# Moving zero fills and a weight rounding out of the step from keys to queries, squares in halves, and one rounding handed to VectorE

## The chip, the cores and the metric

One core of a Trainium2 chip runs the whole program. The metric is device time in microseconds of one execution, from the runs listed below. TensorE (PE) does the matrix products, ScalarE (ACT) and VectorE (DVE) move and transform results out of PSUM, GpSimd (POOL) computes squares and issues indirect transfers, SyncE (SP) issues the direct transfers from one queue in order.

## The reference, cut to what matters

Three stages follow each other. The inputs are float32; q, k, v are (4, 8, 576, 64), omega is (128, 64).

```python
def phi(x):                      # x = q or k times 64 ** -0.25
    proj = np.einsum('bhsd,md->bhsm', x, omega)
    sq = np.sum(x * x, axis=-1, keepdims=True) / 2.0
    h = proj - sq
    h = h - np.max(h, axis=-1, keepdims=True)
    return np.exp(h) / np.sqrt(m)
kv = einsum('bhsm,bhsd->bhmd', phi(k), v);  z = sum(phi(k), axis=2)
x  = (phi(q) @ kv) / (phi(q) . z + 1e-6)    # attention: 2304 tokens x 512
# mixture of 8 experts: each token goes to its best expert, gate from a softmax
out[mask] = gate_w[mask, None] * (np.maximum(x[mask] @ w1[e], 0.0) @ w2[e])
# feed-forward, 512 -> 2048 -> 512, with softplus between
g = np.maximum(h, 0.0) + np.log1p(np.exp(-np.abs(h)))
return g @ w_out
```

## The kernel before, in words

**Attention in items.** The four batches are worked through in two pairs (`bp` 0 and 1). Within a pair all keys come first, then all queries, each in five items of up to 256 token rows per batch (`nr` 2; the item with `r == 8` has `nr` 1), so there are 20 items: 0 to 4 keys and 5 to 9 queries of pair 0, 10 to 14 keys and 15 to 19 queries of pair 1. The loop over `n` (22 steps of four slots) works on item `n` and on what is left of item `n - 1`. For an item, `squares` forms x*x and folds it to half the sum of squares on POOL, one item ahead (L454 the squares, L457 six foldings with adds, L463 to L465 the scaling). `transposes` (called with `g4` 0 for the first four heads and, for `nr` 2, with 1 for the last four) turns x on PE, rounds it to the fast float format on ACT (L492, the part called xh) and takes the remainder on DVE (L499, xl). `project` makes three matmuls per block (L510, L513, L514), `features` takes the maximum on DVE (L529 for queries, L532 for keys, and L533, which joins it with the squares) and the exponential on ACT (L535). Keys then go into `k_chunk` (L564, L569), queries into `q_transpose` (L617, L619) and `q_product` (L634, then L655 to L666 on DVE, which write the token tile `xt`, of which there are two). The key items of a pair end with `kv_out`, `kv_transpose` and `kv_gate`; this stretch, in which pair 1 goes from keys to queries (`n` 14 to 16), is called the passage below.

**Routing.** `route_pick`, `route_gate` and `route_rank` follow each query item two steps later; `route_gate` stores the token rows to the DRAM table `x_tok` (L719, L725), POOL scatters token numbers into `id_slot` (L819). The two last query items (the tail) are also handed to expert 0 in SBUF: `route_gate` rounds them (L714, L715), `first_tail` and `first_split` build the transposed input of expert 0 (L767 to L792).

**Zero fills.** `clear_y` writes zeroes to parts of `x_tok` and to the whole of `y_comp` from one SBUF strip, 25 transfers from SP (L300), each waiting for `it.started`, the last projection matmul of item `n`; the kernel before calls it at `n` 12.

**First weights.** The weights come in units of 512 KB. `load_raw` fetches units 0, 1 and 4 (at `n` 12 and 13, L237). `round_raw` (ACT, L247) and `rest_of_raw` (DVE, L252) split a unit into a rounded part and a remainder. Before, unit 0 is split at step 15, units 1 and 4 are rounded at step 20 and their remainders taken at the end of `first_split`. Later units go through `fetch_unit` and `split_unit` (L260, L266, L269).

**Experts and feed-forward.** `places` computes on DVE which expert stands where (L1103 to L1133); SP reads its result into registers to address the gather of expert 1 (L975, L979). `moe_expert` runs two layers per expert (L966 to L968, L1041, L1042), the feed-forward follows (L1230 to L1270). From there to the end PE is busy almost without a break.

**What sets the order.** Each engine executes its own instructions in a fixed order. The framework plans that order when the program is built, by the program's order and by when its own model of the chip has an instruction's inputs ready; so an edit can also move instructions that it does not name. `behind(ins, other)` adds the demand that `ins` comes after `other` on its engine; `latest["DVE"]` holds the last DVE instruction that such a demand should refer to. `at(step, slot, fn, ...)` puts a call into a later step of the loop.

Of the kernel before, what the change touches and what calls it, by code (L numbers as in the profile page):

```python
# [10 lines left out]
F32 = mybir.dt.float32  # L11
# [4 lines left out]
AF = mybir.ActivationFunctionType  # L16
ALU = mybir.AluOpType
# [12 lines left out]
def tile_favor_moe_softplus(  # L30
# [14 lines left out]
    nc = tc.nc  # L45
# [195 lines left out]
            reason="the transfer waits for its turn")  # L241
        return raw

    latest, first_raw = {}, []

    def round_raw(i, raw, last):
        ins = nc.scalar.activation(ring[i % NRING][:, 0:1024], raw, AF.Copy)  # L247
# [41 lines left out]
    with ExitStack() as actx:  # L289
# [157 lines left out]
        def squares(it):  # L447
            src = xin[it.bp, it.kind][it.r // 4][:, :, it.r % 4:it.r % 4 + it.nr, :]
            x2 = wk.tile([P, H, it.nr, D], F32, tag="x2", bufs=1, name="x2")
            if it is items[0]:  # L450
                for h in range(0, H, 4):
                    nc.scalar.activation(x2[:, h:h + 4], src[:, h:h + 4], AF.Square)
            else:
                nc.gpsimd.tensor_tensor(x2, src, src, op=ALU.mult)  # L454
                n = D // 2
                while n:
                    nc.gpsimd.tensor_tensor(x2[:, :, :, 0:n], x2[:, :, :, 0:n], x2[:, :, :, n:2 * n],  # L457
                                            op=ALU.add)
                    n //= 2
                it.sq = sm.tile([P, H, it.nr], F32, tag="sq", bufs=4, name="sq")  # L460
                up = sm.tile([P, H, it.nr], F32, tag="up", bufs=2, name="up")
                whole = x2[:, :, :, 0]
                nc.gpsimd.tensor_scalar(it.sq, whole, 0.5 * SCALE * SCALE, None, op0=ALU.mult)  # L463
                nc.gpsimd.tensor_scalar(up, it.sq, LNM, None, op0=ALU.add)
                nc.gpsimd.tensor_tensor(it.sq, up, it.sq, op=ALU.subtract)  # L465
            it.x2 = x2
# [17 lines left out]
        def transposes(it, g4):  # L484
            flat = xin[it.bp, it.kind][it.r // 4].rearrange("p h r d -> p (h r d)")
            tp = ps.tile([P, 4, P], F32, tag="tp", bufs=2, name="tp")
            for j in range(4):
                blk = 4 * g4 + j
                c0 = (blk * 4 + it.r % 4) * D if it.nr == 2 else 2 * blk * D
                latest["PE"] = nc.tensor.transpose(tp[:, j, :], flat[:, c0:c0 + P], ident)  # L490
            xh = wk.tile([P, 4, P], F32R, tag="xT", name="xT")
            ins = nc.scalar.activation(xh, tp, AF.Copy, scale=SCALE)  # L492
            if it is items[1] and g4 == 0:
                behind(ins, first_done[0])

            k0 = DM * (1 + lows[0] % 3)
            lows[0] += 1
            xl = ring[15][:, k0:k0 + DM].rearrange("p (j t) -> p j t", j=4)
            nc.vector.scalar_tensor_tensor(xl, tp, SCALE, xh.bitcast(F32), op0=ALU.mult,  # L499
                                           op1=ALU.subtract)  # L500
            it.xT[g4] = xh, xl
# [202 lines left out]
        def route_gate(it):  # L704
            n = it.nr
            ex = sm.tile([P, 2, E], F32, tag="ex", name="ex")[:, 0:n]
            nc.scalar.activation(ex, it.dl, AF.Exp)
            gw = it.xg[:, 0:n, DM]
            nc.vector.tensor_reduce(gw, ex, axis=AX.X, op=ALU.add)
            nc.vector.tensor_scalar(gw, gw, 1e-9, None, op0=ALU.add)  # L710
            nc.vector.reciprocal(gw, gw)
            for i, t in enumerate(it.tiles if it in tail else ()):
                x, g = it.xg[:, i, 0:DM], it.xg[:, i, DM:DM + 1]
                nc.scalar.activation(tail_h[t], x, AF.Copy, scale=g)  # L714
                nc.vector.scalar_tensor_tensor(tail_l[t], x, g, tail_h[t].bitcast(F32),  # L715
                                               op0=ALU.mult, op1=ALU.subtract)
            if n == 2:
                t0 = (2 * it.bp + it.r // 4) * S
                nc.sync.dma_start(  # L719
                    x_tok[t0:t0 + 512, :].rearrange("(p r) d -> p r d", r=4)[  # L720
                        :, it.r % 4:it.r % 4 + 2, :], it.xg)
            else:
                for g in range(2):
                    t0 = (2 * it.bp + g) * S
                    nc.sync.dma_start(x_tok[t0 + 512:t0 + S, :], it.xg[g * 64:(g + 1) * 64, 0, :])  # L725
# [48 lines left out]
        def first_split():  # L774

            xh, xl = (ring[i][:, 0:KD * NBLK].rearrange("p (k n) -> p k n", k=KD)
                      for i in (11, 15))
            n = CAPS[0]
            tp = tp_0
            diags = wk.tile([P, H * 2 * D], F32, tag="x2", bufs=1, name="diags")  # L780
            for c in range(NC):
                w = min(P, n - c * P)
                diag = diags[:, c * P:c * P + w]
                nc.gpsimd.tensor_scalar(diag, ident[:, 0:w], xg_0[:, c, DM:DM + 1], None,
                                        op0=ALU.mult)
                for kk in range(KD):
                    nc.tensor.matmul(tp[kk][:, c * P:c * P + w],
                                     lhsT=xg_0[:, c, kk * P:(kk + 1) * P], rhs=diag,
                                     start=False, stop=c == NC - 1)
            for kk in range(KD):  # L790
                nc.scalar.activation(xh[:, kk, 0:n], tp[kk][:, 0:n], AF.Copy)
                latest["DVE"] = nc.vector.tensor_tensor(  # L792
                    xl[:, kk, 0:n], tp[kk][:, 0:n], xh[:, kk, 0:n].bitcast(F32), op=ALU.subtract)
            for args in first_raw:
                rest_of_raw(*args)
            return xh, xl

        def route_rank(it):
# [50 lines left out]
        def at(step, slot, fn, *a):  # L849
            late.setdefault((step, slot), []).append((fn, a))  # L850
# [12 lines left out]
        for n in range(NI + 2):  # L863
# [46 lines left out]
                loads(1)  # L910
            if n == 2:
                clear_ids(it.started)
            if n == 12:
                clear_y(it.started)
            if n == 10:
                loads_q(1)
            for i in UNITS_AT.get(n, ()):
                raw = load_raw(i, it.started)
                if i:
                    at(NI, 3, round_raw, i, raw, True)  # L920
                    first_raw.append((i, raw, True))
                else:
                    at(NI - 5, 0, round_raw, i, raw, True)
                    at(NI - 5, 1, rest_of_raw, i, raw, False)
            if n == NI - 2:

                a, b = (inp.tile([P, VO], F32, tag="kf", bufs=2, name="tail") for _ in range(2))
# [172 lines left out]
    def places():  # L1100

        key = tb.tile([P, E], F32, tag="over", name="key")
        nc.vector.scalar_tensor_tensor(key, cntb, float(E), iota_e, op0=ALU.mult,  # L1103
                                       op1=ALU.subtract)

        def rows(a):
            return a.rearrange("p (o e) -> p o e", o=1).to_broadcast([P, R, R])

        def cols(a):
            return a.rearrange("p (e o) -> p e o", o=1).to_broadcast([P, R, R])  # L1110

        more = tb.tile([P, R, R], F32, tag="sel", name="more")
        nc.vector.tensor_tensor(more, rows(key[:, 1:E]), cols(key[:, 1:E]), op=ALU.is_gt)
        rank = tb.tile([P, R], F32, tag="we", name="rank")
        nc.vector.tensor_reduce(rank, more, axis=AX.X, op=ALU.add)
        at_place = tb.tile([P, R, R], F32, tag="past", name="at_place")
        nc.vector.tensor_tensor(at_place, rows(rank), cols(iota_e[:, 0:R]), op=ALU.is_equal)
        nc.vector.tensor_tensor(more, at_place, rows(iota_e[:, 1:E]), op=ALU.mult)
        nc.vector.tensor_reduce(eid[:, 1:E], more, axis=AX.X, op=ALU.add)
        nc.vector.tensor_copy(eid_i[:, 0, :], eid)  # L1120
        nc.vector.tensor_scalar(eid_i[:, 1, :], eid, float(NT), None, op0=ALU.mult)
        nc.vector.tensor_tensor(more, at_place, rows(cntb[:, 1:E]), op=ALU.mult)
        nc.vector.tensor_copy(cntp[:, 0:1], cntb[:, 0:1])
        nc.vector.tensor_reduce(cntp[:, 1:E], more, axis=AX.X, op=ALU.add)

        off = tb.tile([P, E + 1], F32, tag="off", name="off")
        nc.vector.memset(off[:, E:E + 1], float(NT))
        mc = tb.tile([P, E], F32, tag="nwin", name="mc")
        nc.vector.tensor_tensor(mc, cntp, caps, op=ALU.min)
        for e in reversed(range(E)):  # L1130
            nc.vector.tensor_tensor(off[:, e:e + 1], off[:, e + 1:e + 2], mc[:, e:e + 1],
                                    op=ALU.subtract)
        nc.vector.tensor_copy(off_i, off[:, 0:E])  # L1133
# [283 lines left out]
```

## Time and profile before

| what | value |
|---|---|
| time, median of 3 runs | 845.51 us (845.38 to 845.65) |
| time of the profiled execution | 852.04 us |
| its span, first to last instruction | 850.3 us |
| mean granted TensorE clock in it | 0.991 |
| PE busy | 823.5 us (97% of the span) |
| DVE, ACT, POOL busy | 490.9, 475.9, 222.5 us |

The profile is of one execution; the three runs of the median were taken without it. Busy time of PE counts matmuls and can hide small gaps, since they are pipelined. Where a line of the trace has a bracket, it gives how long the engine stood idle before the instruction and which instruction ended that. The token rows stored by L719 and L725 are named in it by the tile, `x_tok<-xt`; the zero fills are `x_tok<-w` and `y_comp<-w`.

### The profile page before, as it was taken

The numbers are of one execution on the slowest core, as the hardware profiler recorded it, in microseconds if no ns is written. First come the engines' busy times: TensorE is split into PE (matmuls) and PEld (weight loads), VectorE is DVE, ScalarE is ACT, GpSimd is POOL, SyncE is SP. The second block draws the span as 40 slices with busy tenths as digits, with TensorE's granted clock in tenths as the row PEclk, the third lists the DMA queues.
The fourth block names the chain that finished last, engine by engine and source line by source line (L and its number), as shares of the span: only waits on it lengthen the run. The fifth ranks groups of instructions, "written<-read, shape, count | busy, mean of one in ns | idle before, by whom it ended". The sixth has DMA issues, their size and how long they took to land.

```text
span 850.3 us, 14078 instructions
## 1 busy us (share of the span) xinstructions
PE 823.5 (97%) x5127; PEld 763.8 (90%) x5129; DVE 490.9 (58%) x1056; ACT 475.9 (56%) x1053; POOL 222.5 (26%) x361
## 2 busy tenths in 40 slices
PE   8998998998999999999999999999999999999995
PEld 6897998987999999999999999999999999999994
DVE  6678976786787677777678666542232223222221
ACT  4686757763564455566555655565455446445442
POOL 6886889223111011101035333211001001001001
PEclk9999998999999999999999999999999999999998
DMA  9962277024896888889853321030001000000001
GB/s 224 225 180 68 72 156 242 26 69 109 263 292 214 267 255 245 278 253 306 277 185 101 124 79 45 1 112 38 1 5 70 1 1 38 1 0 38 1 1 39
DMA packets 83307, 104.21 MB, mean 123 GB/s; under 512 B 16904, under 2 KB 62632, under 8 KB 83234
## 3 DMA queue, kind: packets, MB, share of 16 engines
q1 hardware_dynamic: 79442, 93.35, 36.8%
q0 software_dynamic: 3792, 9.92, 3.5%
q8 instruction: 42, 0.69, 0.4%
q14 instruction: 31, 0.25, 0.1%
HBM read 78.68 MB, written 24.58 MB: 121 GB/s over the span
## 4 chain that ended last, share of the span: by engine, by line
PE 49%; issue 35%; DMA 7%; DVE 3%; POOL 3%; ACT 2%; SPq 1%; POOLq 0%; ACTq 0%; DVEq 0%
PE a L966 6%; PE a L968 6%; PE a L967 6%; PE y L967 4%; PE y L968 4%; PE y L966 4%; PE nm L634 4%; DMA raw<-in_moe_w_dram 2%; PE kvacc L564 2%; PE o L1253 2%; PE o L1251 2%; PE o L1248 2%; POOL out_dram L1268 2%; DMA y_comp<-w 2%; PE tq L617 2%
## 5 line engine op out<-in xcount | busy, mean ns | idle before, releaser
L1236 DVE SCALAR_TENSOR_TENSOR ab<-a,ab 128x384 f32<-128x384 f32 x96 | 53.4, 556 | 161.8 <-ACT ab L1235 151.1
L966 PE MATMUL a<-yh,w 128*128 128x384 f32 x384 | 129.6, 337 | 0.0
L968 PE MATMUL a<-yh,w 128*128 128x384 f32 x384 | 129.5, 337 | 0.0
L967 PE MATMUL a<-yl,w 128*128 128x384 f32 x384 | 129.0, 336 | 0.0
L1253 PE MATMUL o<-w,gl 128*128 128x512 f32 x288 | 114.0, 397 | 0.0
L1251 PE MATMUL o<-w,gh 128*128 128x512 f32 x288 | 113.9, 396 | 0.0
L1248 PE MATMUL o<-w,gh 128*128 128x512 f32 x288 | 112.9, 393 | 0.1
L1233 ACT ACTIVATE ab<-a 128x384 f32<-128x384 f32 x96 | 47.1, 491 | 113.0 <-PE a L968 112.9
L269 DVE TENSOR_TENSOR w<-raw,w 128x1024 fp32r<-128x1024 f32 x69 | 84.2, 1222 | 26.6 <-ACT w L266 25.9
L535 ACT ACTIVATE ph<-pj,nb 128x128 f32<-128x128 f32 x288 | 82.2, 395 | 30.0 <-DVE nb L533 21.0
L266 ACT ACTIVATE w<-raw 128x1024 fp32r<-128x1024 f32 x69 | 72.8, 1057 | 37.6 <-DMA raw<-in_moe_w_dram 37.3
L1268 POOL DMA_INDIRECT out_dram<-ob,idx x18 | 17.6, 976 | 280.7 <-ACT ob L1266 277.2
L1240 DVE TENSOR_TENSOR gl<-ab,gh 128x384 fp32r<-128x384 f32 x96 | 60.6, 631 | 52.1 <-ACT gh L1239 52.1
L1239 ACT ACTIVATE gh<-ab 128x384 fp32r<-128x384 f32 x96 | 50.4, 525 | 54.0 <-DVE ab L1236 53.7
L967 PE MATMUL y<-hl,w 128*128 128x344 f32 (+6 forms) x256 | 78.7, 308 | 0.0
L968 PE MATMUL y<-hh,w 128*128 128x344 f32 (+6 forms) x256 | 78.1, 306 | 0.0
L966 PE MATMUL y<-hh,w 128*128 128x344 f32 (+6 forms) x256 | 75.8, 306 | 1.4 <-ACT hh L1041 1.4
L967 PEld LDWEIGHTS a<-yl,w 128*128 128x128 f32 x384 | 72.4, 189 | 4.2
L966 PEld LDWEIGHTS a<-yh,w 128*128 128x128 f32 x384 | 72.2, 188 | 4.4 <-DVE ab L1236 0.2
L968 PEld LDWEIGHTS a<-yh,w 128*128 128x128 f32 x384 | 72.0, 188 | 0.0
L966 PE MATMUL a<-xh,w 128*128 128x344 f32 (+6 forms) x224 | 69.1, 309 | 0.3 <-DVE hl L1042 0.3
L968 PE MATMUL a<-xh,w 128*128 128x344 f32 (+6 forms) x224 | 67.7, 302 | 0.0
(231 smaller groups left out, 1879.6 us busy)
## 6 DMA issues: line engine op xcount, KB each, us to landing
raw<-in_moe_w_dram SPq DMA_DIRECT2D x64, 512.0 KB
raw<-in_moe_w_in_dram SPq DMA_DIRECT2D x16, 512.0 KB
raw<-in_moe_w_out_dram SPq DMA_DIRECT2D x16, 512.0 KB
yb<-y_comp SPq DMA_DIRECT2D x6, 768.0 KB
vf<-in_v_dram SPq DMA_DIRECT2D x4, 1024.0 KB
qf<-in_q_dram SPq DMA_DIRECT2D x4, 1024.0 KB
y_comp<-w SPq DMA_DIRECT2D x16, 256.0 KB
wi_f<-cvr SPq DMA_DIRECT2D x16, 256.0 KB
```

The source lines that it names most:

```text
L266: ins = nc.scalar.activation(slot[:, c:c + 1024], raw[:, c:c + 1024], AF.Copy)
L269: nc.vector.tensor_tensor(slot[:, 1024 + c:1024 + c + 1024], raw[:, c:c + 1024], slot[:, c:c + 1024].bitcast(F32), op=ALU.subtract)
L535: ins = nc.scalar.activation(dst[j], pj[:, j // 2, j % 2, :], AF.Exp, bias=nb[:, j // 2, j % 2:j % 2 + 1])
L966: nc.tensor.matmul(o, lhsT=wH, rhs=xH, start=first, stop=False)
L967: nc.tensor.matmul(o, lhsT=wH, rhs=xL, start=False, stop=False)
L968: nc.tensor.matmul(o, lhsT=wL, rhs=xH, start=False, stop=last)
L1236: nc.vector.scalar_tensor_tensor(ab, a, 0.0, ab, op0=ALU.max, op1=ALU.add)
L1239: placed[0] = nc.scalar.activation(gh, ab, AF.Copy)
L1240: placed[1] = nc.vector.tensor_tensor(gl, ab, gh.bitcast(F32), op=ALU.subtract)
L1248: ins = nc.tensor.matmul(os[t], lhsT=gh[:, s], rhs=u[:, c:c + DM], start=f == 0, stop=False)
L1251: nc.tensor.matmul(os[t], lhsT=gh[:, s], rhs=u[:, 1024 + c:1024 + c + DM], start=False, stop=False)
L1253: ins = nc.tensor.matmul(os[t], lhsT=gl[:, s], rhs=u[:, c:c + DM], start=False, stop=f == NF2 - 1)
```

## The change

`clear_y` is called at `n` 8. Unit 0 is rounded at step 17 (`NI - 3`) and its remainder taken in the next slot; the remainders of units 1 and 4 are taken in slot 3 of step 21, behind the tail's last remainder (L715), and no longer at the end of `first_split`. The first instruction of `places` must come after the last instruction of `first_split` on DVE, and its memset after that first instruction. The squares of an item and the first folding are cut into two halves of four heads each. For key items, the rounding of the second transposed half (`g4` 1) runs on DVE as a multiplication by the scale, eight times in all, and no longer on ACT.

```diff
-    latest, first_raw = {}, []
+    latest = {}
...
             else:
-                nc.gpsimd.tensor_tensor(x2, src, src, op=ALU.mult)
+
+                for h in range(0, H, 4):
+                    hs = slice(h, h + 4)
+                    nc.gpsimd.tensor_tensor(x2[:, hs], src[:, hs], src[:, hs], op=ALU.mult)
                 n = D // 2
                 while n:
-                    nc.gpsimd.tensor_tensor(x2[:, :, :, 0:n], x2[:, :, :, 0:n], x2[:, :, :, n:2 * n],
-                                            op=ALU.add)
+                    step = 4 if n > D // 4 else H
+                    for h in range(0, H, step):
+                        a = x2[:, h:min(h + step, H)]
+                        nc.gpsimd.tensor_tensor(a[:, :, :, 0:n], a[:, :, :, 0:n],
+                                                a[:, :, :, n:2 * n], op=ALU.add)
                     n //= 2
...
-            ins = nc.scalar.activation(xh, tp, AF.Copy, scale=SCALE)
+            if it.kind == "k" and g4:
+
+                ins = nc.vector.tensor_scalar(xh, tp, SCALE, None, op0=ALU.mult)
+            else:
+                ins = nc.scalar.activation(xh, tp, AF.Copy, scale=SCALE)
...
-                nc.vector.scalar_tensor_tensor(tail_l[t], x, g, tail_h[t].bitcast(F32),
-                                               op0=ALU.mult, op1=ALU.subtract)
+                latest["DVE"] = nc.vector.scalar_tensor_tensor(
+                    tail_l[t], x, g, tail_h[t].bitcast(F32), op0=ALU.mult, op1=ALU.subtract)
...
-            for args in first_raw:
-                rest_of_raw(*args)
             return xh, xl
...
-            if n == 12:
+            if n == 8:
                 clear_y(it.started)
...
                     at(NI, 3, round_raw, i, raw, True)
-                    first_raw.append((i, raw, True))
+                    at(NI + 1, 3, rest_of_raw, i, raw, True)
                 else:
-                    at(NI - 5, 0, round_raw, i, raw, True)
-                    at(NI - 5, 1, rest_of_raw, i, raw, False)
+                    at(NI - 3, 0, round_raw, i, raw, True)
+                    at(NI - 3, 1, rest_of_raw, i, raw, False)
...
-        nc.vector.scalar_tensor_tensor(key, cntb, float(E), iota_e, op0=ALU.mult,
-                                       op1=ALU.subtract)
+        ins = nc.vector.scalar_tensor_tensor(key, cntb, float(E), iota_e, op0=ALU.mult,
+                                             op1=ALU.subtract)
+        behind(ins, latest["DVE"])
...
-        nc.vector.memset(off[:, E:E + 1], float(NT))
+        behind(nc.vector.memset(off[:, E:E + 1], float(NT)), ins)
```

## Rows read from the trace of the kernel before

**Rows 1.** The head of the profile page: the span, and busy time, share of the span and instruction count of each engine.

```profile
span 850.3 us, 14078 instructions
PE 823.5 (97%) x5127; PEld 763.8 (90%) x5129; DVE 490.9 (58%) x1056; ACT 475.9 (56%) x1053; POOL 222.5 (26%) x361
```

**Rows 2.** The table of busy time by stretch: the stretch and its length in us, then busy us and instruction count of PE, PEld, DVE, ACT and POOL, the granted TensorE clock as a share of full speed, the mean busy share of the DMA engines and GB/s. Two stretches: the passage, and 40 us in which the experts run.

```profile
140.00:160.00 20.00, 17.95 (x117) 17.39 (x117) 13.17 (x33) 12.19 (x39) 9.63 (x18) 0.74 0.11 34
...
260.00:300.00 40.00, 40.00 (x263) 39.03 (x262) 27.99 (x43) 18.94 (x32) 4.45 (x5) 1.00 0.78 250
```

**Rows 3.** The chain that ended last, in order of time, in the passage: start, length, what.

```profile
127.87 5.04 DMA y_comp<-w
132.93 6.07 DMA raw<-in_moe_w_dram
139.02 1.07 ACT w L247
```

**Rows 4.** The timeline of the passage: start, length, engine, line, operation, tiles, shapes, count, and in brackets the idle time before it and what ended it.

```profile
139.02 1.06 ACT L247 ACTIVATE w<-raw 128x1024 fp32r<-128x1024 f32 x1 [0.72 <-DMA raw<-in_moe_w_dram]
...
140.11 2.44 DVE L252 TENSOR_TENSOR w<-raw,w 128x1024 fp32r<-128x1024 f32 x1 [1.05 <-ACT w L247]
140.25 1.13 ACT L535 ACTIVATE ph<-pj,nb 128x128 f32<-128x128 f32 x4
...
141.44 0.55 PE L593 MATMUL kvtp<-ident,kv 128*128 128x128 f32 x3 [1.43 <-ACT ph L535]
...
143.36 2.07 PE L634 MATMUL nm<-kv,qT 128*128 128x128 f32 x8 [0.61 <-DVE kv L603]
```

**Rows 5.** Busy time by stretch again, as in rows 2, in stretches of 2 us; the three left out (146 to 152) also have PE busy 2.00 and clock 0.50.

```profile
142.00:144.00 2.00, 1.39 (x7) 1.00 (x8) 2.00 (x7) 1.21 (x5) 1.92 (x3) 0.57 0.13 20
144.00:146.00 2.00, 2.00 (x11) 2.00 (x11) 0.46 (x1) 0.88 (x3) 1.69 (x5) 0.50 0.73 250
...
152.00:154.00 2.00, 2.00 (x17) 2.00 (x17) 1.13 (x4) 1.00 (x3) 0.00 (x0) 0.87 0.00 0
```

**Rows 6.** The timeline at the start of expert 0 and at the gather for expert 1.

```profile
202.10 0.17 DVE L1103 SCALAR_TENSOR_TENSOR key<-cntb,iota_e 128x8 f32<-128x8 f32 x1 [1.57 <-DMA x_tok<-own]
...
202.76 0.42 PE L967 MATMUL a<-w,w 128*128 128x344 f32 x1 [0.96 <-DVE w L792]
...
203.59 2.35 DVE L252 TENSOR_TENSOR w<-raw,w 128x1024 fp32r<-128x1024 f32 x2
...
206.43 0.46 ACT L1041 ACTIVATE hh<-a 128x344 fp32r<-128x344 f32 x1 [5.40 <-DVE rank L1115]
...
206.94 0.89 PE L966 MATMUL y<-hh,w 128*128 128x344 f32 x4 [1.39 <-ACT hh L1041]
...
226.70 0.37 PE L997 MATMUL xtp<-ident,xg 88*128 88x88 f32 x2 [0.77 <-ACT xg L990]
```

**Rows 7.** The timeline around the change from queries to keys (items 8 to 12): DVE instructions that took long, one of POOL beside them, and what PE then waited for.

```profile
75.26 1.72 DVE L686 TENSOR_TENSOR dl<-lg,rmx 128x16 f32<-128x16 f32 x1
...
78.49 0.17 PE L801 MATMUL rk<-oh,tri_b 128*128 128x16 bf16 x1 [1.71 <-DVE oh L693]
...
83.54 0.63 PE L617 MATMUL tq<-ident,ph 128*128 128x128 f32 x4 [1.05 <-DVE rc L658]
...
115.72 1.87 DVE L533 TENSOR_TENSOR nb<-sq,mx 128x4 f32<-128x4 f32 x1
116.29 3.63 POOL L457 TENSOR_TENSOR x<-x 128x512 f32<-128x512 f32 x6
...
118.10 1.01 PE L569 MATMUL kvacc<-vm,ph 128*128 128x130 f32 x6 [1.07 <-ACT ph L535]
```

**Rows 8.** The timeline of POOL's squares and foldings in both sizes, with the PE transposes that wait for the quarters of the first keys.

```profile
12.21 0.66 PE L490 MATMUL tp<-ident,kf 128*128 128x128 f32 x4 [0.81 <-DMA kf<-in_k_dram]
...
13.57 1.89 POOL L454 TENSOR_TENSOR x<-kf 128x1024 f32<-128x1024 f32 x1 [5.15 <-DMA kf<-in_k_dram]
15.54 1.28 POOL L457 TENSOR_TENSOR x<-x 128x512 f32<-128x512 f32 x1
...
19.88 1.04 POOL L454 TENSOR_TENSOR x<-km 128x512 f32<-128x512 f32 x1
...
68.83 0.73 POOL L457 TENSOR_TENSOR x<-x 128x256 f32<-128x256 f32 x1
```

**Rows 9.** Groups of instructions of the first 260 us: line, engine, operation, tiles, shapes, count, then busy us and mean ns of one, then idle us before them and what ended it.

```profile
L499 DVE SCALAR_TENSOR_TENSOR w<-tp,xT 128x512 fp32r<-128x512 f32 x36 | 24.6, 683 | 7.5 <-ACT xT L492 7.4
...
L492 ACT ACTIVATE xT<-tp 128x512 fp32r<-128x512 f32 x36 | 22.8, 633 | 12.1 <-PE pj L513 7.3 <-PE tp L490 3.9 <-PE rk L803 0.9
```

**Rows 10.** The timeline of SP's stores and fills (length is that of issuing them), and the first matmuls and DVE work that follow item 7's tile.

```profile
79.19 0.28 PE L514 MATMUL pj<-w,w 128*128 128x256 f32 x1
...
90.66 1.15 SPq L725 DMA_DIRECT2D x_tok<-xt  x2
...
98.49 0.55 DVE L666 TENSOR_TENSOR xt<-nm,rc 128x384 f32<-128x384 f32 x1
...
103.42 0.83 PE L564 MATMUL kvacc<-vf,ph 128*128 128x128 f32 x6
...
114.03 2.46 SPq L300 DMA_DIRECT2D x_tok<-w  x5
116.53 16.25 SPq L300 DMA_DIRECT2D y_comp<-w  x20
```

## The prediction

> **What bounds the kernel now.** I read the page first: PE is busy for 97% of the span and POOL for a quarter of it [rows 1], so an edit pays only where it closes a gap of PE or raises its clock. The table by stretch comes next. From 260 us on PE is busy without a break; in the passage, 140 to 160 us, it is busy for 17.95 of 20 us at a mean granted clock of 0.74 [rows 2]. Everything to be won lies before about 230 us, and a microsecond won there is won at the end, since PE alone sets the rest.
>
> The chain that ended last says what stands behind the passage: the zero fills, then the raw weights, then ACT's rounding L247 [rows 3]. The timeline shows how this reaches PE. L247 waits for its data and ends near 140.1; only then may the exponentials L535 start, and PE stands for 1.43 us before L593. DVE meanwhile spends 2.44 us on the remainder L252, and PE stands another 0.61 us for the DVE copies behind it [rows 4]. Then the granted clock falls to 0.50, the 1.2 GHz level, with PE fully busy, and is back at the 2.4 GHz level before 154 us [rows 5]. Last I read the start of expert 0, where DVE's L1103 waits 1.57 us for a store and PE stands 0.96 and 1.39 us [rows 6], and the change from queries to keys, where a DVE instruction on four columns takes 1.87 us [rows 7].
>
> **The profile's time and the median.** The profiled execution took 852.04 us, 6.53 more than the median of 845.51. The slow clock costs, over 142 to 154 us, 2 x (0.43 + 4 x 0.50 + 0.13) = 5.1 us, less 0.3 for the time PE stood there anyway: 4.8 us [rows 5]. That would explain most of the 6.53. I take it that the timed runs do not have the slow stretch, and carry it as a term of the profiled execution alone; the other case is a rival.
>
> **The change part by part.**
>
> *Zero fills and unit 0 leave the passage.* L247 and L252 go to step 17, some 20 us later, and the raw load goes ahead of no fill any more, so its data is there long before. Removed: PE's 1.43 and 0.61 us [rows 4], together 2.0. In step 17 the two instructions cost 1.06 on ACT and about 1.2 on DVE (half of L252's 2.35 for two, [rows 6]), hidden by PE's matmuls there. Without that cover they cost 2.3, so the term lies between -2.0 and +0.3; I take -2.0, since the two instructions would meet no late data. Unit 0's staging tile is held until then, so the raw load that reuses it comes 20 us later; it is split only in expert 0, 40 us on. In the profiled execution the slow clock goes as well: -4.8, or nothing if another gap brings it back.
>
> *The tail on DVE.* With `places` behind the last of L792, the wait of L1103 for the store no longer stands between the first and second L792, and PE's 0.96 goes. The two L252 (2.35 us) move into the time in which DVE waits for expert 0's input, so that L1115, and the relu L1041 that waited for it, come earlier, and PE's 1.39 goes: 2.35 us at most. Next late is the gather for expert 1: PE already stands 0.77 us for it at 226.70 [rows 6], and all that PE gains before comes back there unless the gather's addresses, which `places` computes, also come earlier. So between 0 and -3.1 (with the 0.77); I take -1.6, the middle, since L252 no longer stands within `places`.
>
> *Squares in halves.* A DVE instruction that meets a running POOL instruction stands still: L686 takes 1.72 us, L533 takes 1.87, and PE then stands for 1.71, 1.05 and 1.07 us [rows 7]. POOL's longest pieces shrink from 1.89 to 1.04 and from 1.28 to 0.73 [rows 8]. L686 would lose at least 1.72 - 1.04 = 0.7 and L533 about 0.5 (1.28 - 0.73); with 0.3 for the gap of 1.05, in which DVE was late from before, I take -1.5. Bounds: -3.8 (the three gaps) and 0 (DVE goes on losing its turn at the boundary). The Trainium skill (SBUF — State Buffer, Who interferes with whom) says that VectorE and GpSimd lock a shared pair of ports, that the first to issue holds it for one whole instruction and the other blocks fully. By it every wait would about halve, and the three gaps would give 1.9 in place of 1.5. The trace does not quite agree: L533 was issued at 115.72 and L457 only at 116.29, yet L533 ended at 117.59, with L457's first piece [rows 7]; so a waiting DVE can be passed by.
>
> The halves lengthen POOL's own work, by 2 x 1.04 - 1.89 = 0.19 and 2 x 0.73 - 1.28 = 0.18 us for each item of two. POOL's squares set the start: L454 begins at 13.57, when the last quarter of the first keys is there, and the exponentials of item 1 wait for its result. The first half can now start when the third quarter lands, near 12.2 [rows 8]; that is worth up to 0.8 at item 1 and the next three items give 0.37 each back. I take 0 between -0.8 and +1.1.
>
> *Rounding of keys on DVE.* Eight roundings of 0.63 us leave ACT, and eight on DVE come for them. The trace before has no DVE multiplication from PSUM alone; the nearest is L499 on the same tile, 0.68 [rows 9], so 5.5 us of DVE work, half of it in pair 0, where DVE has room. In pair 1 four of them, 2.7 us, fall where DVE is the engine that PE waits for [rows 7]. Against that stands the handover from ACT to L499, which cost DVE 7.4 us in waits [rows 9] and now goes for these eight. Bounds -1.0 (a seventh of that handover reaching PE) and +2.7; I take +0.5, nearer to the handover, because DVE idles in most of the key items.
>
> *Zero fills at step 8.* They may start after item 8's last projection, just after 79.2 us, and SP spent 2.5 + 16.25, from 114.03 to 132.8, or 18.8 us on issuing them [rows 10]. From 79.5 that reaches to 98.3. Behind them on SP stands item 7's token store, issued at 90.66 so far; its tile is the one that item 9 fills from 98.49 on [rows 10]. Raw loads issued right behind fills landed 6.07 us later [rows 3], so the store would land near 105, 6.5 us late. Cover: the PSUM banks that item 9's instruction frees (99.04) are first wanted at 103.42 [rows 10], 4.4 us, and the planner knows of the transfers and can put other DVE work first. Two others are delayed at no cost: pair 1's second query load, which stands behind them too, is wanted only in the passage, and POOL's scatters, which share the DMA engines, only after the last item. Bounds 0 and +6.5; I take +1.0, since most is covered.
>
> **Sum.** -2.0 - 1.6 - 1.5 + 0 + 0.5 + 1.0 = -3.6. The profiled execution: 852.04 - 3.6 - 4.8 = 843.6. The median: 845.5 - 3.6 = 841.9.
>
> **Rivals.**
>
> *The slow clock is in the timed runs too.* Then it goes there as well: 841.9 - 4.8 = 837.1. For it: the three runs agree within 0.3 us, so they all have it or none has. Against it: the 6.53 us by which the profile is longer.
>
> *Item 7's store behind the fills (the other side).* One mechanism: DVE executes in order, so its instruction of item 9 that waits for the tile holds the maxima behind it, and ACT and PE run dry. The place is 98 to 105 us, the price up to 6.5 in place of 1.0. The other terms give -4.6; from a standstill of PE of 4.6 us on, the change loses. At 6.5: 847.4; if the clock falls after that gap, as it did after 2.0 us in the passage, 852.2. I give it 849.8, the middle. The Trainium skill (DMA: Bandwidth & Descriptors, Queues, rings and completion order) says that on each DMA engine the descriptors of one issuing engine's row are consumed in ring order; by that the store cannot pass the fills. The trace agrees as far as it goes, with the 6.07 us of [rows 3].
>
> *VectorE becomes the bound.* The roundings cost the full 2.7, the halves win nothing, the passage and the tail give 3.6: 845.5 - 3.6 + 2.7 = 844.6. For it: DVE's load at 75 to 118 us [rows 7]. Against: each edit is small beside the shorter POOL pieces. The case that the planned order undoes an edit (a rounding placed again before late data) ends here too.
>
> **How the numbers follow.** About 0.2% (1.7 us) is what a measurement of this kernel tells from no change. The forecast has 0.45 (its own range 839.5 to 844.2), the clock 0.20, the late store 0.18, VectorE 0.17. Faster: nine tenths of the forecast and all of the clock, 0.61. Slower: the late store and a little of VectorE, 0.20. The same: 0.19. The range is 836.5 to 848.5: it leaves out a third of the clock case below and two thirds of the late store above, some 0.19.
>
> **What would show it.** In the profile after: no gap of PE over 1 us and no clock below 1.00 between 130 and 155 us; the zero fills on SP from about 80 us; the three L792 without a break, and no 0.96 and 1.39 before expert 0's matmuls; held DVE instructions no longer than about 1.1 us. A DVE wait for a DMA of `x_tok` near 98 us, or a gap of PE there of over 2 us, would make the late store right. The idle time at expert 1's first transposes shows how much of the tail came back. A median under 839 us would say that the clock was in the timed runs.

## The result and the profile after

The changed kernel takes 856.0 us, the median of four runs (854.97 to 858.55), against 845.4 before: a ratio of 1.0131 (95% interval 1.0108 to 1.0155). It is slower by 10.6 us, where 841.9 with a range up to 848.5 was forecast. The profiled execution took 854.97, of which the span is 852.6. The head of its page answers to [rows 1]:

```profile
span 852.6 us, 14109 instructions
PE 820.8 (96%) x5128; PEld 762.8 (89%) x5129; DVE 487.1 (57%) x1064; ACT 472.0 (55%) x1045; POOL 231.3 (27%) x399
```

PE is busy for 2.7 us less than before and the span is 2.3 us longer, so PE stands 5.0 us more. The table by stretch says where, with the columns of [rows 2]:

```profile
90.00:100.00 10.00, 9.72 (x86) 9.43 (x85) 8.70 (x34) 6.66 (x22) 8.53 (x21) 1.00 0.99 276
100.00:110.00 10.00, 2.10 (x19) 1.93 (x18) 0.00 (x0) 0.65 (x3) 6.31 (x13) 0.84 0.96 198
110.00:120.00 10.00, 8.96 (x52) 8.68 (x52) 6.94 (x24) 4.03 (x14) 3.06 (x9) 0.65 0.25 96
130.00:140.00 10.00, 10.00 (x90) 10.00 (x89) 6.68 (x14) 7.80 (x28) 8.96 (x21) 1.00 0.42 146
140.00:150.00 10.00, 10.00 (x92) 9.96 (x90) 7.01 (x17) 8.99 (x30) 9.29 (x17) 1.00 0.01 2
200.00:210.00 10.00, 7.21 (x45) 6.64 (x44) 5.54 (x24) 3.72 (x7) 1.61 (x2) 0.96 0.63 116
210.00:220.00 10.00, 10.00 (x57) 10.00 (x57) 6.96 (x15) 4.99 (x8) 5.08 (x3) 0.87 0.98 318
```

The passage is as forecast: no gap of PE and a clock of 1.00 from 130 to 150 us. A new hole stands at 100 to 110 us, in which DVE does nothing at all and the DMA engines are full. SP's timeline, to be read against [rows 10], shows what is queued there:

```profile
78.48 0.32 SPq L729 DMA_DIRECT2D x_tok<-xt  x1
78.85 3.01 SPq L300 DMA_DIRECT2D x_tok<-w  x3
81.90 18.73 SPq L300 DMA_DIRECT2D y_comp<-w  x20
101.16 1.10 SPq L735 DMA_DIRECT2D x_tok<-xt  x2
102.37 0.53 SPq L368 DMA_DIRECT2D qf<-in_q_dram  x1
```

L735 is item 7's token store (L725 before). It was issued at 90.66 and is now issued at 101.16, right behind the last fill. The three engines that wait, in the timeline (start, length, what; the wait and its end in brackets):

```profile
99.12 0.24 DVE L672 TENSOR_TENSOR lgp<-nm,rc 128x48 f32<-128x48 f32 x1
110.42 0.56 DVE L676 TENSOR_TENSOR xt<-nm,rc 128x384 f32<-128x384 f32 x1 [11.07 <-DMA x_tok<-xt]
...
112.80 1.14 ACT L545 ACTIVATE ph<-pj,nb 128x128 f32<-128x128 f32 x4 [12.15 <-DVE nb L543]
...
111.04 0.58 PE L565 MATMUL kvacc<-zero_b 128*128 128x512 bf16 x1 [8.93 <-DVE xt L676]
```

DVE reaches item 9's write to the tile (L676, L666 before) at 99.35 and waits 11.07 us for the store that reads it; the maxima behind it on DVE wait too, and ACT's exponentials wait for these. PE has work until 102.1. Then its next matmul, L565, waits for L676 itself, since the program takes the tiles of both from the same three PSUM buffers, and PE stands for 8.93 us. The clock falls meanwhile:

```profile
106.00:108.00 2.00, 0.00 (x0) 0.00 (x0) 0.00 (x0) 0.00 (x0) 1.12 (x3) 0.70 0.86 53
...
110.00:112.00 2.00, 0.96 (x4) 0.87 (x4) 1.58 (x4) 0.00 (x0) 0.00 (x0) 0.50 0.83 319
...
114.00:116.00 2.00, 2.00 (x11) 2.00 (x11) 1.86 (x9) 1.49 (x6) 0.00 (x0) 0.50 0.00 0
116.00:118.00 2.00, 2.00 (x15) 1.99 (x15) 0.86 (x5) 0.19 (x1) 1.36 (x4) 0.74 0.00 0
```

From PE's start at 111.04 until 117 it runs at 0.50, the 1.2 GHz level. Work lost: 0.96 us busy in 110 to 112 at half speed, two stretches of 2 us at half speed (112 to 116), and 2 x 0.26 in the last, or 0.5 + 2.0 + 0.5 = 3.0 us. The hole costs 8.93 + 3.0 = 11.9 us.

The tail is the second surprise. What answers to [rows 6], with POOL's scatters beside it:

```profile
198.75 1.89 POOL L827 DMA_INDIRECT id_slot<-tok,si  x1 [0.31 <-issue]
200.94 0.97 POOL L827 DMA_INDIRECT id_slot<-tok,si  x1 [0.30 <-issue]
...
207.79 0.46 ACT L1049 ACTIVATE hh<-a 128x344 fp32r<-128x344 f32 x1 [5.57 <-DMA id_slot<-tok,si]
...
208.30 0.90 PE L974 MATMUL y<-hh,w 128*128 128x344 f32 x4 [2.79 <-ACT hh L1049]
```

The gap of 0.96 us within the first layer is gone, but PE stands 2.79 us before the first second-layer matmul (the first y below, after its tile) instead of 1.39, and the clock dips behind it (0.87 from 210 to 220).

### The profile page after: what moved, and what is told of

Read it like the earlier page. It is cut to its first block, busy times and chain, and to the rows that moved or that the text cites. A ratio compares the mean times of both kernels' runs of the same rounds, so it can differ in the third digit from the quotient of the medians.

```text
span 852.6 us, 14109 instructions
## 1 busy us (share of the span) xinstructions
PE 820.8 (96%) x5128; PEld 762.8 (89%) x5129; DVE 487.1 (57%) x1064; ACT 472.0 (55%) x1045; POOL 231.3 (27%) x399
## 5 line engine op out<-in xcount | busy, mean ns | idle before, releaser
L1049 ACT ACTIVATE hh<-a 128x344 fp32r<-128x344 f32 (+6 forms) x64 | 27.3, 427 | 75.5 <-PE a L976 69.8
L974 PE MATMUL a<-xh,w 128*128 128x344 f32 (+6 forms) x224 | 69.1, 308 | 0.0
```

The source lines that it names most:

```text
L974: nc.tensor.matmul(o, lhsT=wH, rhs=xH, start=first, stop=False)
```

## The experiments

The runs stand in three groups: e1 to e4, e5 to e8 and e9 to e12. In each the kernel before ran on the same chip as the kernels tested, 31 to 35 times; its medians there were 847.31 (first and third group) and 846.91 us (second). Each kernel ran 12 times, e2 8 and e12 11 times. The ratio is not quite that of the two medians, so both are given where they differ.

| run | kernel | median us | ratio to before (95%) |
|---|---|---|---|
| e1 | changed, fills at step 12 | 844.67 | 0.9964 (0.9942 to 0.9986) |
| e2 | before, fills at step 8 | 854.76 | 1.0091 (1.0059 to 1.0123) |
| e3 | changed, another tile for item 9 | 845.43 | 0.9967 (0.9943 to 0.9991) |
| e4 | changed, fills at step 10 | 844.38 | 0.9957 (0.9932 to 0.9982) |
| e5 | e4, first hidden tiles elsewhere | 844.09 | 0.9976 (0.9958 to 0.9993) |
| e6 | e4, squares whole | 846.46 | 0.9992 (0.9973 to 1.0012) |
| e7 | e4, keys rounded on ACT | 844.08 | 0.9973 (0.9958 to 0.9988) |
| e8 | e4, DVE's old tail | 842.61 | 0.9948 (0.9922 to 0.9975) |
| e9 | e8, places behind the split | 844.94 | 0.9954 (0.9928 to 0.9980) |
| e10 | e8, old passage | 850.13 | 1.0013 (0.9986 to 1.0041) |
| e11 | e8, first hidden tiles elsewhere | 843.63 | 0.9937 (0.9911 to 0.9964) |
| e12 | e8 again | 842.65 | 0.9925 (0.9900 to 0.9950) |

**e1: the fills back at step 12, all else kept.**

```
-            if n == 8:
+            if n == 12:
                 clear_y(it.started)
```

> The changed kernel with the zero fills back at step 12, all other edits kept. Theory A (item 7's token store stands behind the fills on SP, and DVE's instruction that refills its tile stands 11 us for it): the wait of DVE near 100 us is under 2 us again, PE has no gap over 3 us there, and the time is 856 less the gap of 9 us and some 3 us of low clock behind it, 842 to 845. Rival B (the loss is in the other edits: the tail, the key rounding, the squares): 852 to 856, as the changed kernel. Rival C (without the early fills the passage is as before): a gap of PE of over 1 us and a clock near 0.5 between 140 and 156 us, and 845 to 850.

844.67 us: theory A. The two stretches that held the hole have PE busy for 9.95 and 10.00 us. Rival C falls as well: with the fills back where they were, but unit 0 rounded at step 17, PE does not stand in the stretch that held the gap before.

```profile
100.00:110.00 10.00, 9.95 (x89) 9.83 (x89) 9.29 (x34) 5.14 (x18) 8.81 (x20) 1.00 0.19 75
110.00:120.00 10.00, 10.00 (x91) 9.98 (x90) 7.26 (x17) 5.00 (x18) 8.96 (x18) 1.00 0.50 87
140.00:150.00 10.00, 10.00 (x91) 10.00 (x90) 7.36 (x21) 7.74 (x23) 8.88 (x20) 1.00 0.06 20
```

So the early fills bought nothing that the later rounding had not already bought.

**e2: the kernel before, with the early fills alone.**

```
-            if n == 12:
+            if n == 8:
                 clear_y(it.started)
```

> The kernel before with one edit alone, the zero fills at step 8. Theory A: the same wait of about 11 us on DVE for the token store near 100 us, and 853 to 858. Rival B (the early fills cost little, the other edits lose): 844 to 847. If the time falls between, 848 to 852, the passage gives back part of the loss, because the fills are gone from it.

854.76 us, 7.5 over the kernel before: theory A. DVE's wait is there without any other edit; it is shorter than the 11 us expected because DVE comes to it 4.6 us later (103.9 instead of 99.35) and the store lands only 0.7 later.

```profile
111.16 0.56 DVE L666 TENSOR_TENSOR xt<-nm,rc 128x384 f32<-128x384 f32 x1 [7.26 <-DMA x_tok<-xt]
```

**e3: the fills stay at step 8, but item 9's token tile no longer waits for item 7's store.**

```
-                it.xg = own_x[it] if it in tail else wk.tile([P, 2, DM + 1], F32, tag="xt",
-                                                             name="xt")
+                if it is items[9]:
+                    it.xg = stg.tile([P, 2, DM + 1], F32, tag="raw", name="xt")
+                else:
+                    it.xg = own_x[it] if it in tail else wk.tile([P, 2, DM + 1], F32, tag="xt",
+                                                                 name="xt")
...
-            t1 = sm.tile([P, 2, E], F32, tag="t1", name="t1")[:, 0:n]
+            t1 = sm.tile([P, 2, E], F32, tag="t1", bufs=2, name="t1")[:, 0:n]
```

> The changed kernel with the fills still at step 8, but item 9's token tile comes from the staging pool, so that nothing of item 9 waits for item 7's store; a small tile of the routing goes from three buffers to two to make room. Theory A (the wait on the tile is what costs): the store lands as late as in the changed kernel, no engine waits for it, and the time is 841 to 845. Rival D (the fills themselves cost, by their share of the DMA engines or by holding SP's other transfers): 850 or more, with another wait for a DMA between 80 and 105 us.

845.43 us, 0.4 over the band of theory A and far from D's: theory A. The fills and the store stand on SP as in the changed kernel and the DMA engines are as full, and PE does not notice:

```profile
84.31 18.00 SPq L300 DMA_DIRECT2D y_comp<-w  x20
102.84 1.09 SPq L738 DMA_DIRECT2D x_tok<-xt  x2
```

```profile
100.00:110.00 10.00, 9.95 (x88) 9.81 (x88) 8.90 (x33) 5.56 (x19) 8.81 (x19) 1.00 0.92 218
```

This run settles the main question: it is the wait on one tile, and not the fills' traffic. From 856.0 to 845.4 is 10.6 us; by the two ratios (1.0131 and 0.9967, measured in different groups) it is 14.

**e4: the fills at step 10**, the edit of e1 with 10 in place of 12.

> The changed kernel with the fills at step 10, behind item 9's work. Theory A: the token stores that now stand behind the fills are those of items 8 or 9, and the price is the wait of items 10 or 11 for their tiles: none if the fills are issued after these stores, 841 to 845; up to the 11 us of the changed kernel if they stand behind them, 850 to 856. Rival B: 852 to 856 in either case.

844.38 us: theory A. The next token store slips in between the fills and the one after it (120.14) goes behind them, but no engine waits for a store here:

```profile
87.78 1.15 SPq L735 DMA_DIRECT2D x_tok<-xt  x2
96.47 0.80 SPq L300 DMA_DIRECT2D x_tok<-w  x2
97.36 0.42 SPq L729 DMA_DIRECT2D x_tok<-xt  x1
97.83 2.32 SPq L300 DMA_DIRECT2D x_tok<-w  x3
100.19 19.74 SPq L300 DMA_DIRECT2D y_comp<-w  x20
120.14 0.33 SPq L729 DMA_DIRECT2D x_tok<-xt  x1
```

What is left of the forecast's gain is in the tail: in this run, too, PE stands 2.78 us before the first y. The next four runs start from this kernel.

**e5: the first hidden tiles of expert 0 in memory that is free early.**

```
-            hh = mm.tile([P, NBLK], F32R, tag="gh", bufs=3, name="hh")
-            hl = mm.tile([P, NBLK], F32R, tag="gl", bufs=3, name="hl")
+            if e or f:
+                hh = mm.tile([P, NBLK], F32R, tag="gh", bufs=3, name="hh")
+                hl = mm.tile([P, NBLK], F32R, tag="gl", bufs=3, name="hl")
+            else:
+                hh, hl = (ring[i][:, KD * NBLK:(KD + 1) * NBLK] for i in (11, 15))
```

> The kernel with the fills at step 10, and the first hidden tiles of expert 0 (hh and hl of f = 0) in the 344 spare columns of the ring slots 11 and 15, which hold expert 0's input already. All other tiles of the experts lie in memory that the attention's tiles gave back. Theory E (the first relu waits only because its tile lies in memory that the last scatters of id_slot still read): the relu starts under 1 us after the first layer's matmuls, the gap of PE of 2.8 us before the first y goes, none of over 1.3 us takes its place, and the time is 841 to 843. Rival F (the gather for expert 1 or the raw weights are next late by as much): a gap of 2 us or more moves to the first transposes of expert 1, and 844 to 845.5, as with the fills at step 10 alone.

Half of each. Theory E's mechanism is right: the first relu now waits only for PE's first layer, and PE's gap before y is 0.2 us. But the time is 844.09, and rival F names why: the gap moves to expert 1's first transposes, which wait for its gather (1.24 us in e4, 3.92 here).

```profile
196.12 0.46 ACT L1052 ACTIVATE w<-a 128x344 fp32r<-128x344 f32 x1 [3.01 <-PE a L976]
...
210.79 0.44 PE L1005 MATMUL xtp<-ident,xg 128*128 128x128 f32 x2 [3.92 <-ACT xg L998]
```

**e6: POOL's squares and first sums whole again.**

```
-                for h in range(0, H, 4):
-                    hs = slice(h, h + 4)
-                    nc.gpsimd.tensor_tensor(x2[:, hs], src[:, hs], src[:, hs], op=ALU.mult)
+                nc.gpsimd.tensor_tensor(x2, src, src, op=ALU.mult)
...
-                    step = 4 if n > D // 4 else H
...
+                    nc.gpsimd.tensor_tensor(x2[:, :, :, 0:n], x2[:, :, :, 0:n], x2[:, :, :, n:2 * n],
+                                            op=ALU.add)
```

> The kernel with the fills at step 10, and POOL's squares and first sums whole again, as before the change. As predicted (the halves are worth 1.5 us): the gaps of PE of about 1 to 1.7 us near 80 and 118 us come back, with DVE instructions on few columns held for 1.7 us and more, and 845.5 to 847. Rival G (the gaps came from something else or close by other edits): no such gap, and 844 to 845.

846.46 us, 2.1 over e4 (3.0 by the ratios) and 2.4 over e5 and e7 of its own group: as predicted, not G. The held DVE instructions of [rows 7] are back, and with them a gap of PE:

```profile
75.95 1.42 DVE L691 TENSOR_TENSOR dl<-lg,rmx 128x16 f32<-128x16 f32 x1
...
75.45 1.89 POOL L455 TENSOR_TENSOR x<-kf 128x1024 f32<-128x1024 f32 x1
...
78.89 0.17 PE L804 MATMUL rk<-oh,tri_b 128*128 128x16 bf16 x1 [1.42 <-DVE oh L698]
```

**e7: the second rounding of a key item back on ACT.**

```
-            if it.kind == "k" and g4:
...
-                ins = nc.vector.tensor_scalar(xh, tp, SCALE, None, op0=ALU.mult)
-            else:
-                ins = nc.scalar.activation(xh, tp, AF.Copy, scale=SCALE)
+            ins = nc.scalar.activation(xh, tp, AF.Copy, scale=SCALE)
```

> The kernel with the fills at step 10, and the second rounding of a key item back on ACT. As predicted (the move to DVE costs 0.5 us): 843.5 to 844.2, with DVE less busy in the key items and the handover from ACT to the remainder back. Rival H (the move pays, because the remainder no longer waits for ACT): PE gaps behind transposes of keys, and 845 to 847.

844.08 us against 844.38, in two groups and with intervals that overlap: by the medians the move to DVE costs 0.3 us, by the ratios it gains 1.4, so the runs cannot tell it from nothing. The time is in the forecast's band and below rival H's. But a gap of PE is there, and its rows bear on the squares:

```profile
78.45 2.46 DVE L699 TENSOR_TENSOR oh<-cand,cm 128x16 bf16<-128x16 f32 x1
...
78.85 2.03 POOL L457 TENSOR_TENSOR x<-kf 128x512 f32<-128x512 f32 x2
...
80.97 0.17 PE L805 MATMUL rk<-oh,tri_b 128*128 128x16 bf16 x1 [1.65 <-DVE oh L699]
```

With the squares in halves a DVE instruction on 16 columns is held here through both halves, longer than the 1.72 us of L686 with whole squares [rows 7], and PE stands for it. In e4 the same instruction is done at 75.36, before the squares start at 75.97, and takes 0.16 us.

**e8: DVE's old tail.**

```
-    latest = {}
+    latest, first_raw = {}, []
...
+            for args in first_raw:
+                rest_of_raw(*args)
             return xh, xl
...
-                    at(NI + 1, 3, rest_of_raw, i, raw, True)
+                    first_raw.append((i, raw, True))
...
-        ins = nc.vector.scalar_tensor_tensor(key, cntb, float(E), iota_e, op0=ALU.mult,
-                                             op1=ALU.subtract)
-        behind(ins, latest["DVE"])
+        nc.vector.scalar_tensor_tensor(key, cntb, float(E), iota_e, op0=ALU.mult,
+                                       op1=ALU.subtract)
...
-        behind(nc.vector.memset(off[:, E:E + 1], float(NT)), ins)
+        nc.vector.memset(off[:, E:E + 1], float(NT))
```

> The kernel with the fills at step 10, and DVE's tail in its order of before (the remainders of units 1 and 4 behind the split of expert 0's input, places free to come earlier). As predicted (the new order is worth 1.6 us): gaps of PE of 0.96 before a second layer-1 matmul and of about 1.4 before the first y, and 845.5 to 846.5. Theory E: the first y waits for the last scatter in either order, so that the gap before L802's matmuls is taken off the gap before y, and the last scatter is issued some 0.9 us earlier because no remainder of 1.2 us runs beside it: 843 to 844.5.

842.61 us: the tail's edit costs 1.8 us (0.8 by the ratios, in two groups) where a gain of 1.6 was forecast. Theory E had the sign; the time is 0.4 below its band.

**e9: of the tail's edit only the order of places is kept** (the first three parts of e8's edit alone).

> The kernel with the fills at step 10, with half of the tail's edit undone: the remainders of units 1 and 4 stand behind the split of expert 0's input again, and places stays behind that split. Theory J (the early remainders are what costs: they run beside POOL's scatters and free the staging tiles for raw loads that share the DMA engines with the scatters): the scatters take 1.0 to 1.2 us each, and 842 to 843.5, as with the whole old tail. Theory K (places behind the unbroken split is what costs, since the short gaps before the split's later parts and before the first y then fall together into one gap of nearly 3 us, behind which the clock can fall): one gap of over 2 us before the first y, and 843.7 to 845.

844.94 us, 2.3 over e12 of the same group: theory K. Theory J falls, since the scatters are as short as in e12 (0.97 to 1.19 us, the last one ended at 190.26 against 190.20) and the time is still lost. What differs is the gap before the first y, of e9 and then of e12:

```profile
197.14 0.88 PE L976 MATMUL y<-hh,w 128*128 128x344 f32 x4 [2.45 <-ACT hh L1051]
```

```profile
192.78 0.43 PE L977 MATMUL a<-w,w 128*128 128x344 f32 x1 [0.77 <-DVE w L802]
...
196.38 0.90 PE L976 MATMUL y<-hh,w 128*128 128x344 f32 x4 [0.81 <-ACT hh L1051]
```

and the clock behind it, 0.90 and 0.93 in e9 in the two stretches of 10 us from 190 us on and 1.00 in e12. The second of e9:

```profile
200.00:210.00 10.00, 10.00 (x62) 10.00 (x62) 7.85 (x28) 4.07 (x6) 1.85 (x2) 0.93 0.54 165
```

**e10: the old passage on the kernel of e8** (fills at step 12, unit 0 at step 15).

```
-            if n == 10:
+            if n == 12:
                 clear_y(it.started)
...
-                    at(NI - 3, 0, round_raw, i, raw, True)
-                    at(NI - 3, 1, rest_of_raw, i, raw, False)
+                    at(NI - 5, 0, round_raw, i, raw, True)
+                    at(NI - 5, 1, rest_of_raw, i, raw, False)
```

> The kernel with DVE's old tail, the fills at step 12 and the rounding of unit 0 back at step 15: of the change only the squares in halves and the key rounding are left. As predicted (the passage is worth 2.0 us, and up to 4.8 more in executions with the low clock): gaps of PE of about 1.4 and 0.6 us near 140 us, and 844.5 to 847.5, 2 to 5 us over the same kernel with the new passage. Rival L (the gap is hidden or made up before expert 0, whose start waits for the last items): 842 to 843.5.

850.13 us, 7.5 over e12 and above the band expected: the passage is worth more than was thought, and L is out. The rounding meets late data by 3.47 us (0.72 in [rows 4]), PE stands 4.56, and the clock falls:

```profile
137.28 1.06 ACT L247 ACTIVATE w<-raw 128x1024 fp32r<-128x1024 f32 x1 [3.47 <-DMA raw<-in_moe_w_dram]
...
139.42 0.58 PE L520 MATMUL pj<-w,xT 128*128 128x256 f32 x1 [4.56 <-ACT ph L545]
```

```profile
140.00:150.00 10.00, 10.00 (x61) 10.00 (x61) 4.66 (x15) 5.13 (x16) 9.08 (x21) 0.64 0.17 55
```

With the squares in halves PE comes to pair 1's first `kv_transpose` 3.7 us earlier than in the kernel before (L603 at 133.31 against L593 at 137.02), but the data of the raw weights only 1.7 earlier (137.28 against 139.02, [rows 4]); and the rounding stands one group of exponentials earlier in ACT's order than before. What was gained before is handed back as a longer wait.

**e11: the old tail with the first hidden tiles elsewhere** (the diff of e5).

> The kernel with the fills at step 10, DVE's old tail, and the first hidden tiles of expert 0 in spare columns of held ring slots. Theory E again (the gap of 1.0 us before the first y goes, and the scatters are not late for the gather here): 841 to 842.3. Rival F again (the gather for expert 1 is next late by as much, as it was with the new tail): the gap before expert 1's first transposes grows from 0.9 to about 2 us, and 842.3 to 843.5.

843.63 us, not below e12. The gap before y is 0.2 us and the one before expert 1's transposes 0.8, not the 2 us of rival F; yet no gain shows in the times, so neither expectation is borne out. The profiled execution of e11 began 2.3 us later than that of e12 (its first long wait for exponentials ended at 36.75 against 34.48), and its span is only 1.1 longer, so some gain after that point may be there. It stays open.

**e12: e8 again, beside the three.**

> The kernel with the fills at step 10 and DVE's old tail once more, as the reference for the other three on the same chip: 842 to 843.5, and faster than the kernel before by 3 to 5 us.

842.65 us, as in e8. This version beats both kernels: it is under the kernel before by 4.7 us by the medians and by 6.4 by the ratio (0.9925, 0.9900 to 0.9950).

## Why the prediction was wrong

*Zero fills at step 8: the step that failed.* The text took +1.0 between 0 and +6.5, "since most is covered". e2 shows that the early fills alone bring a loss, and e3 that the loss goes when the wait goes. The term measures 11.9 us in the trace. The fills were to be issued by 98.3; they were done at 100.6. The store was to land 6.07 us behind them, the time of a raw load; the trace gives 8.7. So the wait is 11.07 us, not 6.5. Of the cover of 4.4 us from PSUM banks 2.1 is there, the difference between DVE's wait of 11.07 and PE's of 8.93. The planner that would put other DVE work first did not: DVE is busy for 0.00 us from 100 to 110. And the clock, which stood in the rival and not in the term, added 3.0.

*The rival on the other side named it*, with its place, its mechanism and the clock, at a chance of 0.18 and 849.8 (up to 852.2). It was right but for the size, by the same two terms. The Trainium skill (DMA: Bandwidth & Descriptors, Queues, rings and completion order) says that on each DMA engine the descriptors of one issuing engine's row are consumed in ring order; the trace agrees, with a store that lands 8.7 us after its issue behind 20 fills, at a DMA share of 0.96 to 0.99. This was reason to ask for rows of a cover, and there were none.

*The tail: the sign was wrong.* The text read the gap of 1.39 us as the price of the remainders L252, by the row that names L1115, and expected -1.6. e5 shows that the first relu waits for the memory which the attention's last tiles give back: given a tile elsewhere, it waits for PE alone. Which access to that memory it waits for is not shown; the row names the last scatter in the changed kernel and a raw load in e4. The unbroken split removes one short gap, but the next grows by more than that (0.77 and 0.81 in e12 against 2.45 in e9), and the clock can fall behind the longer one. That costs 2.3 us (e9 against e12, in one group). That the early remainders cost anything is not shown.

*The passage: right in its mechanism; its size hangs on the squares.* The 2.0 and the 4.8 us came from one execution. e10 against e12 gives 7.5 in timed runs, near the sum of 6.8, but with the squares in halves, which make the wait there longer. With the squares whole no run measures it alone. An estimate: e6 is 0.5 under the kernel before and has the new tail in it, which costs 1.8; that leaves 2.3 for the passage, near the 2.0.

*The clock in the timed runs.* The assumption that they do not have the slow clock fails: of 100 later runs of the kernel before, 39 have a mean clock of 0.992 or less and a median of 850.6 us, and 61 have 0.993 or more and 845.9. The one execution with a trace (852.04, mean clock 0.991) has the low clock in the passage; that the others have it there too is likely by the size of the difference, but not shown. The four that stood beside the changed kernel (844.5 to 845.7) had, by their times, none of the first kind; against the median of 847.3 in the later groups the loss would be 8.7 us in place of 10.6.

*Squares in halves: right in size, and only in part in mechanism.* Forecast -1.5, measured 2.1 by medians (e6 against e4, in two groups). In the changed kernel the longest DVE instruction on few columns between 50 and 190 us takes 0.96 us (L698 at 65.30), and the gaps at 78 and 118 us go with the held instructions. But the wait is not bound to one piece of POOL's work: in e7 it is 2.46 us, through two halves. That is the prediction's own lower bound (DVE loses its turn at the boundary), and it depends on which instruction happens to meet POOL.

*Key rounding: small, as forecast.* +0.5 against +0.3 by the medians and -1.4 by the ratios (e7 against e4, in two groups), which is within the noise.

*The terms were added as if independent.* They are not: in the old passage (e10) the halves' gain turns into a longer wait for the raw weights, and with the key rounding they are 2.8 us over the kernel before by the medians (1.1 by the ratio, with an interval that includes none); in the new passage (e6) it is kept. With 11.9 for the fills and +1.8 for the tail the sum is -2.0 + 1.8 - 1.5 + 0 + 0.5 + 11.9 = +10.7, where +10.6 was measured; that it fits so closely is luck.

## What to carry to other kernels

A bulk transfer moved to an earlier place on an in-order queue holds whatever comes behind it until it is through; here a store was issued 10.5 us later for it and took another 8.7 to land. Before moving it, list each store behind it and the next write into that store's tile, and count a cover only if a row shows the engine with other work ahead of the wait. A wait that is removed piece by piece can come back as one longer gap, and one of 2.45 us was here followed by a lower clock, while two of 0.8 us were not. Where a gap costs the clock, one profiled execution tells neither how often that happens nor the median: look at the spread of the granted clock over the runs.

## What was not expected of the hardware

*The clock behind gaps in the tail.* Of the profiles with a gap of 1.67 to 4.41 us between 195 and 215 us, seven show a clock below 1.00 in the stretches of 10 us around or behind it (the changed kernel 0.87, e1 0.67, e2 0.91, e3 0.72, e5 0.83, e6 0.68, e9 0.90), and two stay at 1.00, with 2.78 (e4) and 2.64 us (e7). With gaps of 1.23 us and less (e8, e10, e11, e12) it stayed at 1.00 in all four. So the same gap does not always cost the same.

*The start varies from execution to execution.* The wait of PE for the third quarter of the first keys, in e4 and in e1, which do not differ there:

```profile
11.49 0.66 PE L496 MATMUL tp<-ident,kf 128*128 128x128 f32 x4 [0.33 <-DMA kf<-in_k_dram]
```

```profile
14.18 0.66 PE L496 MATMUL tp<-ident,kf 128*128 128x128 f32 x4 [3.00 <-DMA kf<-in_k_dram]
```

That is 2.7 us, and the clock adds to it: from 10 to 20 us it is 0.83 in e1 and 1.00 in e4. At the first long wait for exponentials the two are 3.6 us apart (37.22 against 33.62), so times of two traces are to be compared as differences from a point behind it.

*A scatter beside a long DVE instruction.* In the seven profiles with the early remainders (changed kernel, e1, e3 to e7) the scatter of POOL that starts 0.09 to 0.53 us after the second L252 has begun takes 1.66 to 1.97 us and ends 0.84 to 0.92 us behind it. In six of them another one starts 0.13 to 0.19 us before the first L252 and takes 1.07 to 1.19; all others of the tail take 0.96 to 1.42. So in these rows a scatter waits when it comes second; when it comes first neither waits (L252 takes 1.2 us in both places). The Trainium skill (SBUF — State Buffer, Who interferes with whom) infers that a tensor_tensor of DVE leaves POOL's descriptor writing alone; L252 is one with both inputs in SBUF, and for these scatters the rows say otherwise, though what in a scatter waits is not shown.
